# A retention, mixture and attention kernel: the first half block of the second row is loaded through ScalarE's DMA queue

## The chip, the cores and the metric

The kernel runs on one core of one Trainium2 chip. The metric is the device time of one execution in microseconds (us). The profile is a trace of one execution: PE is TensorE's matmuls and PEld its weight loads, DVE is VectorE, ACT ScalarE, POOL GpSimd; SP is SyncE, which here only issues DMA transfers. A name with a q (SPq, ACTq) is an engine's own sequencer, which among other things issues transfers.

## The reference

Three layers follow one another, all in float32, for 2 batch rows of 768 positions. The change touches the loading of the first.

```python
# 1: retention, 8 heads of 64; gamma[h] = 1 - 2 ** (-5 - h)
for t in range(S):
    state = gamma * state + einsum('bhd,bhe->bhde', k[:, :, t], v[:, :, t])
    y[:, :, t] = scale * einsum('bhd,bhde->bhe', q[:, :, t], state)
# 2: 8 experts, one per position: its own best one, or the one of the position before where local_gate >= 0.5
out[b, s] = p[e] * (maximum(x[b, s] @ w1[e], 0) @ w2[e])
# 3: 4 attention experts (causal), the top 2 of a position added with their weights
out += mask * w * ((softmax(scale * q @ k.T) @ v) @ wo[e])
```

## The kernel before

The positions are cut into 6 chunks of 128. A block n is chunk n // 2 of batch row n % 2, so blocks 0 and 1 are the first chunk of the first and of the second row, and there are 12 blocks. In memory a block is 128 partitions by 2048 floats: transposed queries, transposed keys, keys and values, 512 floats each. It is loaded in two halves of 512 KB by `load_half(n, x)` (line 244): x = 0 gives the transposed queries and keys, into a tile called `blq` in the trace, and x = 1 the keys and values, into `blk`. Each kind has four buffers. Every half is one transfer on SyncE's queue.

At the start the decay rows (`DR`, a tile whose buffer is called `am`) are loaded on ScalarE's queue (line 257); SyncE issues, in this order, the first part of the constants `K`, the first halves of blocks 0 and 1, their second halves, the rest of `K`, the first halves of blocks 2 and 3, the query table `qt`, and the second halves of blocks 2 and 3 (lines 258 to 269):

```python
        nc.scalar.dma_start(DR, drow)
        nc.sync.dma_start(K[:, :KS0], consts[:, :KS0])
        load_half(0, 0)
        load_half(1, 0)
        load_half(0, 1)
        load_half(1, 1)
        nc.sync.dma_start(K[:, KS0:], consts[:, KS0:])
```

From then on the order of every engine's instructions is the order in which they are written. For a block, `scores` (line 307 in the rows) multiplies keys by queries on PE; `fade` (line 311) multiplies the scores by the decay mask on VectorE, in two halves of 64 positions each by partition; `outputs_now` (line 349) multiplies the faded scores by the values; `state` (line 363) adds the products of decayed keys (`decay_k`, line 331, on GpSimd) and values into PSUM; `evacuate` (line 354) and `keep` (line 372) copy results out on ScalarE. From the second chunk on `outputs_past` (line 340) adds what the kept state gives for the queries that `decay_q` (line 325, on GpSimd) has scaled by `qt`. `turn_pair` (line 383) then transposes a chunk's outputs. Blocks 0 and 1 take `scores` and `fade` ahead of the loop, with a filler matmul of zeros (`busy`, line 229) between them; each pass of the loop then does `outputs_now` and `state` for two blocks, and `scores` and `fade` for the next two. A buffer is loaded again when its readers are done, and each transfer signals its landing through one of eight DMA semaphores that are given out in turn, over both queues; a transfer that reuses a semaphore first waits for the one that had it.

The pieces of the expert weights (`wraw`, line 181) are fetched on SyncE's queue from the last passes on, and layers 2 and 3 follow.

Of the kernel before, what the change touches and what calls it, by code (L numbers as in the profile page):

```python
# [108 lines left out]
def kernel(  # L109
# [14 lines left out]
    nc = tc.nc  # L124
# [115 lines left out]
    with tc.tile_pool(name="s1", bufs=2) as s1:  # L240
        XB, QT, KD, QD, AM, XR, XT, LL = {}, {}, {}, {}, {}, {}, {}, {}
        N1 = NC * B

        def load_half(n, x):
            c, b = divmod(n, B)
            XB[n, x] = s1.tile([128, 2, DM], F32, name="blk" if x else "blq", bufs=4)
            a = slice(2 * x, 2 * x + 2)
            nc.sync.dma_start(XB[n, x], blk[c, b].rearrange("p (a n) -> p a n", a=4)[:, a])

        def load_pair(c, x):  # L250
            if c >= NC:
                return
            for b in range(B):
                load_half(c * B + b, x)

        DR = s1.tile([128, H * C], F32, name="am")[0:3, :H * C // 2]
        nc.scalar.dma_start(DR, drow)
        nc.sync.dma_start(K[:, :KS0], consts[:, :KS0])
        load_half(0, 0)
        load_half(1, 0)  # L260
        load_half(0, 1)
        load_half(1, 1)
        nc.sync.dma_start(K[:, KS0:], consts[:, KS0:])
# [259 lines left out]
        with tc.manual_schedule(engines={ENG.PE, ENG.DVE, ENG.Activation, ENG.Pool, ENG.SP}):  # L523
# [82 lines left out]
            c = NC - 1  # L606
# [132 lines left out]
            for x in range(2):  # L739
                n = slice(2 * x, 2 * x + 2)  # L740
# [55 lines left out]
    with tc.tile_pool(name="mx", bufs=2) as mp:  # L796
# [44 lines left out]
        for e in range(E):  # L841
# [21 lines left out]
            for f in range(4):  # L863
# [4 lines left out]
                if N > JOIN:  # L868
                    ph = bank("B", [128, 2, CAP])
                    for a in range(2):  # L870
                        n = slice(a * 128, (a + 1) * 128)
# [6 lines left out]
                else:  # L878
                    hc = hh[:, :, 128:] if N <= 192 else None
                    hs.append((hh, hl, hc))  # L880
                    for a in range(2):
                        n = slice(a * 128, (a + 1) * 128)
# [74 lines left out]
            else:  # L957
# [39 lines left out]
                for x in range(2):  # L997
                    place(1, y1[0], x)
                    place(1, y1[1], x, True)
                    n = slice(2 * x, 2 * x + 2)  # L1000
# [496 lines left out]
```

## Time and profile before

| | us |
|---|---|
| time, median of 3 runs | 390.21 |
| lowest and highest of them | 389.69, 390.74 |
| the profiled execution | 390.05 |
| its span, from the first to the last instruction | 388.3 |
| PE busy | 377.5 |
| VectorE, ScalarE, GpSimd busy | 275.9, 237.8, 124.5 |

The span is cut into 40 slices of 9.7 us on the page; a digit is a busy share in tenths. The profiled execution has 1.75 us outside the span. The chain of work that ended last is followed back from the last instruction to whatever released each step. In the timeline a row gives a start, a duration, the engine, the line, the operation with its tiles (out<-in), a count, and in brackets the idle time of the engine just before with what ended it. In the windows each row gives a stretch, its length, busy us of PE, PEld, DVE, ACT and POOL, the granted PE clock as a share of 2.4 GHz, the mean busy share of the 16 DMA engines and the GB/s that they moved.

### The profile page before, as it was taken

To read this page: it belongs to the slowest core of one execution; us is meant where nothing else is said; L and a number is where in the kernel's file an instruction comes from. 1 tells how busy PE (TensorE), PEld (TensorE's weight loads), DVE (VectorE), ACT (ScalarE), POOL (GpSimd) and SP (SyncE) were. 2 spreads that over 40 slices of the span, in tenths; PEclk is the share of its full clock that TensorE was granted. 3 is DMA by queue.
4 is the path that set the end of the run, shared out by engine and by line. 5 is a ranking of instruction groups with operands and counts; after the bars stand their busy time and mean duration, and the time that the engine had idled before them with its cause. 6 is when DMAs were issued, how large, how long until landed. Compare 5 with 4: busy or idle time off the path is not lost.

```text
span 388.3 us, 8414 instructions
## 1 busy us (share of the span) xinstructions
PE 377.5 (97%) x2944; PEld 331.7 (85%) x2944; DVE 275.9 (71%) x783; ACT 237.8 (61%) x557; POOL 124.5 (32%) x175
## 2 busy tenths in 40 slices
PE   7999998999999999999999999999999999999994
PEld 4899996998979888898988797999889988988772
DVE  5466695885575768778888984478976876678741
ACT  1566764373465657578786882467876766759641
POOL 3744442131503013131310013535445332415420
PEclk9999998999999999999999999999999999999999
DMA  7999957477686776777777672232011101000111
GB/s 252 383 401 329 368 202 245 147 246 227 218 275 209 240 238 236 238 252 236 249 245 250 235 279 70 81 106 55 24 50 38 30 1 56 2 28 29 54 57 62
DMA packets 23609, 67.37 MB, mean 174 GB/s; under 512 B 4469, under 2 KB 4725, under 8 KB 23560
## 3 DMA queue, kind: packets, MB, share of 16 engines
q1 hardware_dynamic: 21010, 59.34, 45.0%
q0 software_dynamic: 2544, 7.42, 5.7%
q8 instruction: 25, 0.41, 0.4%
q14 instruction: 24, 0.20, 0.2%
q10 hardware_dynamic: 6, 0.01, 0.0%
HBM read 56.16 MB, written 11.07 MB: 173 GB/s over the span
## 4 chain that ended last, share of the span: by engine, by line
PE 87%; DMA 4%; DVE 3%; ACT 2%; SPq 1%; issue 1%; ACTq 0%; DVEq 0%
PE C L921 20%; PE B L873 9%; PE C L1073 8%; PE B L885 5%; PE C L1258 5%; PE B L1238 5%; PE A L1182 4%; PE C L1111 4%; PE C L1279 4%; PE A L885 3%; PE B L887 2%; DMA blq<-in_blk_dram 2%; DMA wraw<-in_w_dram 2%; PE C L917 2%; PE C L349 2%; PE A L808 2%
## 5 line engine op out<-in xcount | busy, mean ns | idle before, releaser
L191 DVE TENSOR_TENSOR wlo<-wraw,whi 128x1024 fp32r<-128x1024 f32 x64 | 76.9, 1222 | 15.7 <-ACT whi L186 15.6
L186 ACT ACTIVATE whi<-wraw 128x1024 fp32r<-128x1024 f32 x64 | 65.6, 1050 | 3.7 <-DMA wraw<-in_w_dram 3.7
L943 POOL DMA_INDIRECT x_d<-y,SI x16 | 20.1, 1253 | 128.5 <-ACT y L933 81.0
L1216 POOL TENSOR_SCALAR a<-a,mx,wt 128x128 f32<-128x128 f32 (+5 forms) x48 | 34.1, 720 | 51.3 <-PE B L1238 12.0
L1205 ACT ACTIVATE a<-a,mx 128x128 f32<-128x128 f32 (+5 forms) x48 | 32.2, 670 | 23.0 <-DVE mx L1195 19.6
L921 PE MATMUL C<-whi,hh 128*128 128x512 f32 (+4 forms) x112 | 45.5, 406 | 0.0
L921 PE MATMUL C<-whi,hl 128*128 128x512 f32 (+4 forms) x112 | 44.1, 394 | 0.0
L921 PE MATMUL C<-wlo,hh 128*128 128x512 f32 (+4 forms) x112 | 44.1, 394 | 0.0
L885 PE MATMUL B<-xx,whi 128*128 128x384 f32 (+3 forms) x100 | 31.0, 365 | 0.0
L1238 PE MATMUL B<-K,a 128*128 128x128 f32 x168 | 26.4, 274 | 0.0
L1195 DVE CUSTOM_DVE_ANT_0 a<-A,MR 128x384 f32<-128x384 f32 (+3 forms) x48 | 25.3, 531 | 1.4 <-PE A L1182 0.9
L887 PE MATMUL B<-xx,wlo 128*128 128x192 f32 (+3 forms) x100 | 25.5, 255 | 0.0
L921 PEld LDWEIGHTS C<-whi,hl 128*128 128x128 f32 (+4 forms) x112 | 20.0, 179 | 6.1
L921 PEld LDWEIGHTS C<-wlo,hh 128*128 128x128 f32 (+4 forms) x112 | 20.1, 179 | 5.0
L921 PEld LDWEIGHTS C<-whi,hh 128*128 128x128 f32 (+4 forms) x112 | 20.0, 179 | 4.7
L859 ACT ACTIVATE hh<-t 128x128 fp32r<-128x128 f32 (+4 forms) x56 | 16.3, 318 | 12.1 <-DVE t L891 10.4
L1238 PEld LDWEIGHTS B<-K,a 128*128 128x128 f32 x168 | 19.9, 140 | 2.6 <-issue 0.7
L1182 PE MATMUL A<-ks,qh 128*128 128x256 f32 (+3 forms) x56 | 21.5, 384 | 0.0
L220 POOL DMA_INDIRECT xg<-x_d,GI x14 | 16.0, 1142 | 14.8 <-DVE one L766 10.8
L1258 PE MATMUL C<-at,vv 128*64 128x256 f32 (+1 forms) x204 | 20.6, 347 | 0.0
L885 PEld LDWEIGHTS B<-xx,whi 128*128 128x128 f32 x100 | 18.8, 188 | 0.7
L887 PEld LDWEIGHTS B<-xx,wlo 128*128 128x128 f32 x100 | 19.1, 191 | 0.2
(327 smaller groups left out, 974.4 us busy)
## 6 DMA issues: line engine op xcount, KB each, us to landing
wraw<-in_w_dram SPq DMA_DIRECT2D x64, 512.0 KB, 4.0
blq<-in_blk_dram SPq DMA_DIRECT2D x12, 512.0 KB, 5.6
blk<-in_blk_dram SPq DMA_DIRECT2D x12, 512.0 KB, 10.3
x_d<-xr SPq DMA_DIRECT2D x12, 260.0 KB, 8.2
out_dram<-y SPq DMA_DIRECT2D x12, 256.0 KB, 2.0
xr<-x_d SPq DMA_DIRECT2D x10, 256.0 KB, 2.6
x_d<-ZR SPq DMA_DIRECT2D x2, 260.0 KB, 5.3
wraw<-in_wv_dram SPq DMA_DIRECT2D x1, 520.0 KB
```

The lines of the kernel that those rows point to most:

```text
L186: nc.scalar.activation(hi, raws[i], AF.Copy)
L191: nc.vector.tensor_tensor(out=lo, in0=raws.pop(i), in1=hi.bitcast(F32), op=OP.subtract)
L873: nc.tensor.matmul(ph[:, a, :N], w[:, k, n], x[:, k, :N], start=m == 0, stop=m == 11)
L885: nc.tensor.matmul(pa[:, :, :N], wh[:, k, n], XX[e][:, k, :, :N], start=k == 0, stop=False, skip_group_check=True)
L887: nc.tensor.matmul(pa[:, 1, :N], wl[:, k, n], XX[e][:, k, 0, :N], start=False, stop=k == 3, skip_group_check=True)
L921: nc.tensor.matmul(pys[i][:rows], h[:, a, n], w[:, a, :], start=f == 0 and a == 0 and m == 0, stop=f == 3 and a == 1 and m == 2)
L1073: nc.tensor.matmul(pp, w[:, k, a * 128:(a + 1) * 128], x[:, k, :], start=m == 0, stop=m == 11)
L1182: nc.tensor.matmul(ps[:, :w], qq[b, g, e][:, tq], KS[b, e][:, s0:s0 + w], start=m == 0, stop=m == 1)
L1205: nc.scalar.activation(AA[u][:, :n], AA[u][:, :n], AF.Exp, bias=mx[:, 0, i:i + 1], scale=-1.0, accum_out=mx[:, 1, i:i + 1])
L1216: nc.gpsimd.tensor_scalar(a[:, :n], a[:, :n], mx[:, 1, i:i + 1], WT[b, g][:, i, e:e + 1], op0=OP.mult, op1=OP.mult)
L1238: nc.tensor.transpose(pT[:, s - s0, :], a[:, s * C:(s + 1) * C], ident)
L1258: nc.tensor.matmul(po[j * HD:(j + 1) * HD, r], VV[b, s][:, e * HD:(e + 1) * HD], at[j][:, s, r], start=s == 0, stop=s == ns - 1, skip_grou ...
```

## The change

`load_half` gets a parameter for the queue, with SyncE's as the default, and the call for the first half of block 1 passes ScalarE's.

```diff
-        def load_half(n, x):
+        def load_half(n, x, queue=nc.sync):
             c, b = divmod(n, B)
             XB[n, x] = s1.tile([128, 2, DM], F32, name="blk" if x else "blq", bufs=4)
             a = slice(2 * x, 2 * x + 2)
-            nc.sync.dma_start(XB[n, x], blk[c, b].rearrange("p (a n) -> p a n", a=4)[:, a])
+            queue.dma_start(XB[n, x], blk[c, b].rearrange("p (a n) -> p a n", a=4)[:, a])
...
         load_half(0, 0)
-        load_half(1, 0)
+        load_half(1, 0, nc.scalar)
         load_half(0, 1)
         load_half(1, 1)
```

On ScalarE, the start of the program, as a difference (a + is a row that the changed kernel has):

```order
 L1493 UNCONDITIONAL_BRANCH [waits barrier_Pool_Activation_PE_DVE_SP_release]
 L257 DMA am<-in_drow_dram 3x512
+L248 DMA blq<-in_blk_dram 128x1024
 L354 ACT_TABLE_LOAD
 L354 ACTIVATE xT<-C 128x512 [waits PE_49] x2
```

The load stands behind the decay rows and ahead of the load of the activation table, and waits for nothing.

On SyncE's queue, the first loads before the change (a number tells tiles of one name apart: `blq_95` and `blk_99` are the halves of block 0, `blq_97` and `blk_101` those of block 1, 104 and 110 of block 2, 106 and 112 of block 3, `blq_198` is the first half of block 4; DMAHW0 to DMAHW7 are the eight DMA semaphores):

```order
L258 DMA K_63<-in_consts_dram 128x188
L248 DMA blq_95<-in_blk_dram 128x1024
L248 DMA blq_97<-in_blk_dram 128x1024
L248 DMA blk_99<-in_blk_dram 128x1024
L248 DMA blk_101<-in_blk_dram 128x1024
L263 DMA K_63<-in_consts_dram 128x268
L248 DMA blq_104<-in_blk_dram 128x1024
L248 DMA blq_106<-in_blk_dram 128x1024 [waits DMAHW0_49]
L267 DMA qt_108<-in_qtab_dram 128x512 [waits DMAHW1_49]
L248 DMA blk_110<-in_blk_dram 128x1024 [waits DMAHW2_49]
L248 DMA blk_112<-in_blk_dram 128x1024 [waits DMAHW3_49]
L248 DMA blq_198<-in_blk_dram 128x1024 [waits DMAHW4_49,PE_49]
```

And there after it:

```order
L258 DMA K_63<-in_consts_dram 128x188
L248 DMA blq_95<-in_blk_dram 128x1024
L248 DMA blk_99<-in_blk_dram 128x1024
L248 DMA blk_101<-in_blk_dram 128x1024
L263 DMA K_63<-in_consts_dram 128x268
L248 DMA blq_104<-in_blk_dram 128x1024
L248 DMA blq_106<-in_blk_dram 128x1024 [waits DMAHW0_49]
L267 DMA qt_108<-in_qtab_dram 128x512 [waits DMAHW1_49]
L248 DMA blk_110<-in_blk_dram 128x1024 [waits DMAHW2_49]
L248 DMA blk_112<-in_blk_dram 128x1024 [waits DMAHW3_49]
L248 DMA blq_198<-in_blk_dram 128x1024 [waits DMAHW4_49,PE_49]
```

Only `blq_97` has gone; what follows it moves up by one place and keeps its waits (the semaphores go round over both queues: DMAHW0 is that of the decay rows, DMAHW2 that of `blq_95`, DMAHW3 that of `blq_97`, DMAHW4 that of `blk_99`). PE, VectorE and GpSimd have the same rows in the same order.

## Rows read from the trace of the kernel before

**Rows 1.** The page: PE's busy share by slice, in tenths

```profile
PE   7999998999999999999999999999999999999994
```

**Rows 2.** Chain that ended last: start, us, what, up to 50 us

```profile
0.74 0.40 SPq L258
...
5.01 8.95 DMA blq<-in_blk_dram
...
41.50 8.16 DMA wraw<-in_w_dram
```

**Rows 3.** Timeline of the issuing queues and of ScalarE, 0 to 12 us

```profile
0.73 0.54 ACTq L257 DMA_DIRECT2D am<-in_drow_dram  x1
1.19 0.97 SPq L248 DMA_DIRECT2D blq<-in_blk_dram  x2
...
6.05 0.47 SPq L248 DMA_DIRECT2D blk<-in_blk_dram  x1
...
7.26 0.33 SPq L248 DMA_DIRECT2D blk<-in_blk_dram  x1
...
10.08 0.60 ACT L354 ACTIVATE xT<-C 128x512 f32<-128x512 f32 x1 [7.49 <-PE C L349]
```

**Rows 4.** Windows of the start: the last two numbers are DMA share and GB/s

```profile
1.50:2.00 0.50, 0.50 (x3) 0.19 (x2) 0.29 (x1) 0.50 (x1) 0.50 (x3) 1.00 0.38 82
2.00:2.50 0.50, 0.50 (x3) 0.15 (x1) 0.00 (x0) 0.50 (x1) 0.50 (x3) 1.00 0.66 221
...
2.50:5.50 3.00, 2.90 (x9) 0.58 (x7) 1.24 (x5) 0.09 (x1) 0.47 (x3) 1.00 0.95 210
5.50:10.00 4.50, 3.62 (x49) 2.92 (x49) 3.49 (x8) 0.00 (x0) 1.04 (x1) 1.00 1.02 393
...
12.00:16.00 4.00, 3.35 (x49) 2.93 (x45) 2.03 (x4) 2.79 (x8) 1.79 (x6) 1.00 1.02 406
```

**Rows 5.** Timeline of PE and of its weight loads, 5.5 to 16 us

```profile
6.00 1.16 PE L307 MATMUL A<-blq 64*128 64x128 f32 x16 [0.60 <-DMA blq<-in_blk_dram]
...
7.42 0.97 PEld L307 LDWEIGHTS C<-blq 64*128 64x128 f32 x16 [0.23 <-DMA blq<-in_blk_dram]
...
8.95 1.09 PE L349 MATMUL C<-am,blk 128*64 128x128 f32 x16 [0.37 <-DMA blk<-in_blk_dram]
10.26 1.09 PE L349 MATMUL C<-am,blk 128*64 128x128 f32 x16 [0.21 <-DMA blk<-in_blk_dram]
11.15 1.13 PE L363 MATMUL B<-blk,kd 128*64 128x64 f32 x32
...
14.09 1.16 PE L307 MATMUL C<-blq 64*128 64x128 f32 x16 [0.29 <-DMA blq<-in_blk_dram]
```

**Rows 6.** Timeline of VectorE and of GpSimd, 5 to 19 us

```profile
7.20 1.29 DVE L311 TENSOR_TENSOR am<-A,DT 128x512 f32<-128x512 f32 x2 [0.78 <-PE A L307]
8.61 1.29 DVE L311 TENSOR_TENSOR am<-C,DT 128x512 f32<-128x512 f32 x2
...
10.19 1.05 POOL L331 TENSOR_TENSOR kd<-blk,K 128x512 f32<-128x512 f32 x1 [0.18 <-DMA blk<-in_blk_dram]
...
14.68 2.50 POOL L325 TENSOR_TENSOR qd<-blq,qt 128x512 f32<-128x512 f32 x2 [2.21 <-DMA qt<-in_qtab_dram]
```

**Rows 7.** The page's DMA queues: packets, MB, share of 16 engines

```profile
q8 instruction: 25, 0.41, 0.4%
```

**Rows 8.** Timeline of PE in the second and third pass of the loop

```profile
17.17 1.95 PE L340 MATMUL C<-qd,SB 128*128 128x128 f32 x16
...
22.24 1.16 PE L307 MATMUL A<-blq 64*128 64x128 f32 x16
23.23 1.06 PE L307 MATMUL C<-blq 64*128 64x128 f32 x16
```

**Rows 9.** Windows at 40 us and at 62 to 66 us

```profile
40.00:41.00 1.00, 1.00 (x38) 0.93 (x32) 0.14 (x2) 0.60 (x1) 0.26 (x1) 1.00 0.84 270
62.00:66.00 4.00, 3.80 (x22) 2.56 (x21) 2.20 (x10) 2.34 (x5) 2.01 (x2) 0.57 0.75 273
```

## The prediction

> **What bounds the kernel now.** I read the page first: of the 40 slices all but three show PE busy for 9 tenths or more, and the first, with 7, is the lowest apart from the last [rows 1]. That first slice, about 9.7 us, is where the change lies. Next I read the chain of work that ended last, in order of time. It begins with SyncE's queue issuing its transfers back to back from 0.74 to 5.01 us, goes on with the transfer of a half block from 5.01 us to its landing at 13.96, and from there on it is PE work, beginning with the scores of block 3 at 14.09 [rows 5], until the wait for a weight transfer that is issued at 41.50 us [rows 2]. Read alone, that says "SyncE issues too slowly". Two more views say otherwise.
>
> The timeline of the queues shows what issuing costs: 0.97 us for the two first half blocks, so 0.485 us each, while the engines of the DMA need longer to move them [rows 3]. The windows show that the DMA is saturated: its share of busy time is 0.95 from 2.5 to 5.5 us and 1.02 from 5.5 to 10 and from 12 to 16 us [rows 4]. At the 393 GB/s of 5.5 to 10 us a half block of 524,288 bytes takes 1.33 us. PE's and GpSimd's waits end at that spacing: the halves of blocks 0 and 1 are there by 6.00, 7.42, 8.95 and 10.19 us, and the first half of block 3 by 14.09 [rows 5, 6]. So up to 14.09 us the DMA engines set the pace, not the issue; PE waits for them, last of all 0.29 us before the scores of block 3 [rows 5].
>
> **The change, part by part.** It moves one 512 KB transfer, the first half of block 1, from second place among SyncE's block loads to second place in ScalarE's queue. Nothing is added or removed.
>
> Step 1, ScalarE. Its queue issues the decay rows from 0.73 us for 0.54 us [rows 3]; the order shows the moved issue right behind them and ahead of a table load, which ends at 2.59 us (10.08 less the 7.49 of idling behind it, [rows 3]). No row shows a 512 KB issue on that queue; the bounds are SyncE's 0.33 us (a later one) and the 0.54 us of the small one [rows 3], and I take 0.5. The table load then ends at about 3.1 us. ScalarE's first activation starts at 10.08 us [rows 3], so this costs nothing unless the issue took 7 us.
>
> Step 2, SyncE. Everything behind the moved issue goes out up to 0.485 us earlier, as long as nothing holds it. The order shows what does: from the first half of block 3 on, each load waits for the landing of the transfer eight places ahead of it, counted over both queues. The second half of block 2 waits for the first half of block 0, and goes out at 6.05 us, right after that landing; the second half of block 3 waits for the moved transfer and goes out at 7.26 [rows 3, 5]. If the first half of block 0 lands about 1.2 us later, those two go out at about 7.2 and 7.5 us. Behind them on SyncE's queue is the first half of block 4, which is not held up: it waits for the second half of block 0, on which PE starts at 8.95 [rows 5]. The bytes of block 2's second half cannot move before the first halves of blocks 2 and 3 (14.09 us) have gone by, so 7 us of backlog hides the later issue.
>
> Step 3, who gets the DMA engines. Both queues now offer a half block from about 1.3 us on. If they don't share, the first half of block 0 still lands at 6.00; if they share evenly, both land together at about 7.42, the time at which both had landed before [rows 5]. The nearest row is the queue of instruction loads, which runs on the same engines: 0.41 MB in 0.4% of 16 x 388.3 us is 16.5 GB/s for an engine, against some 25 in the stretches of 393 and 406 GB/s over 16 [rows 4, 7]. It loses speed to the other queue, so I take sharing: 7.2 us, a little before 7.42 because SyncE issues 0.1 us earlier.
>
> The Trainium skill (DMA: Bandwidth & Descriptors, "Issuing engines are not separate DMA queues") says that transfers started by different engines run on the same 16 DMA engines and interleave, and that starting them from several engines saves no more than the issuing time. Applied here, the most that the change could bring would be rival (a) below, and S in step 4 would be near the shared end; the spacing of 1.33 us against 0.485 us in the rows agrees that issuing is the smaller of the two.
>
> Step 4, PE's chain from that landing. Call the start of the scores of block 0 S (6.00 before). The first fade starts 1.20 us later and takes 1.29; the scores of block 1 can follow PE's filler at about S + 1.19 (PE reached them 0.23 us before 7.42) and need 1.19 to their fade, so the second fade starts at S + 2.49, when VectorE is free, and ends at S + 3.78 [rows 5, 6]. From block 1's output matmuls to the state is 0.89 us (10.26 to 11.15) and 1.13 more to the next scores, 2.02 in all; the scores of block 3 follow 0.99 us behind those of block 2 where no data is missing (22.24 to 23.23) [rows 5, 8]. So PE is ready for the scores of block 3 at S + 6.79. They started at 14.09, so **a later landing costs nothing up to S = 7.30**, and one for one beyond. With S = 7.2 PE is ready at 13.99. The cover here is PE's waits for half blocks, of 0.37, 0.21 and 0.29 us among others [rows 5]; they are used up, and what is late next is PE itself.
>
> Step 5, when the last of these loads lands. The bytes before block 3 are the same, so its landing moves only if idle DMA time at the start is filled. From 2.0 to 2.5 us the share is 0.66, idle for 0.17 us; from 1.5 to 2.0 it is 0.38, idle for 0.31 [rows 4]. The bounds are 0 and 0.48; I take 0.17, since the earlier idling lies before the first data of any block. That gives 14.09 - 0.17 = 13.92.
>
> **Sum.** The scores of block 3 start at the later of 13.92 and 13.99: 0.10 us earlier. Between the bounds (S from 6.00 to 7.42, landing 0 to 0.48 earlier) this is from 0.48 earlier to 0.12 later. From there the chain is PE [rows 2], so the shift is carried. At 41.50 us it runs through a weight transfer, whose issue waits for PE's state matmuls; the DMA share of 0.84 at 40 to 41 us says there is no backlog that would swallow it [rows 2, 9]. The transform of block 2's queries waits for a table until 14.68 and ends, for blocks 2 and 3 together, at 17.18; the matmuls that read it start at 17.17 with block 2's own half, so 0.1 us fits [rows 6, 8]. The profiled execution took 390.05 us (388.3 span), 0.16 below the median of 390.21: 390.05 - 0.10 = 389.95, and for a median 390.1.
>
> **Rivals.** (a) *The issue does bound the start*, as the chain of waits reads: all that follows goes out 0.485 us earlier and lands so, with S at or below 6.8. For it: the chain. Against it: the DMA share near 1. It gives 389.7.
> (b) *Two queues hide each other's slow packets.* From 2.5 to 5.5 us the engines are 0.95 busy but move 210 GB/s, against 393 later [rows 4]. If the second queue fills that, 3.0 x (1 - 210/393) = 1.4 us are gained and the scores of block 3 start near 12.7, which PE can follow (S = 5.9 gives 12.69): 388.8. Against it: the engines are shown busy, not idle, in that stretch, and the moved bytes go through the same ones.
> (c) *Slower: sharing delays block 0's half past 7.30 us.* Place: the scores of block 0. It decides from S = 7.30 and costs 1 us per us. If three half blocks shared the engines until 8.95 us, S is 8.95 and the loss 1.65: 391.9. For it: the slow packets of 2.5 to 5.5 us may grow with a second stream. A loss over 1.17 us needs S above 8.47.
> (d) *The transfer is not ahead where it should be*: ScalarE's queue is served behind SyncE's, so block 1's half lands after the fourth, at 10.19. Then its scores start 2.77 us later, its fade ends at 12.67 instead of 9.90, and scores of block 3 start at 12.67 + 2.02 + 0.99 = 15.68, a loss of 1.6: 391.8. Against it: the instruction queue's packets do get their share.
>
> **How the numbers follow.** About 0.3% (1.17 us) is what a measurement can tell from no change. Chances: forecast 62%, (a) 14%, (b) 8%, (c) 13%, (d) 3%. Forecast, (a) and the lower two thirds of (c) are within 0.3%; (b) is faster; the upper end of (c) and (d) are slower. That is 8% faster, 86% same, 6% slower. Runs of the kernel before went from 389.69 to 390.74, half a us either way, so the range takes (a) at 389.7 less 0.4 and the lower half of (c) at about 391: 389.3 to 391.0. Left out are (b), (d) and the upper part of (c).
>
> **What would show it.** In the profile after: ScalarE's issue at about 1.3 us for 0.5; the scores of block 0 starting near 7.2 instead of 6.00 and those of block 1 about 1.2 later without a wait; output matmuls of block 1 near 11 instead of 10.26; scores of block 3 within 0.3 us of 14.09. Scores of block 0 still at 6.00 would refute the sharing; scores of block 3 before 13.5 us would mean (a) or (b); after 15 us (c) or (d). The clock is granted at half (1.2 GHz) for a part of 62 to 66 us, the mean being 0.57 [rows 9]; if that stretch changed its length, the time would change for a reason outside this argument.

## The result and the profile after

The changed kernel takes 393.67 us (median of 7 runs, the fastest 390.42), the kernel before 390.21 (7 runs, 389.69 to 391.79): slower by 0.63%, the ratio being 1.0063 with an interval of 1.0042 to 1.0085. One run of 532.09 us, whose mean granted clock was 0.66, is not in the ratio, and without it the median is 393.15 us. 390.1 with a range of 389.3 to 391.0 had been forecast, so the forecast was wrong: 0.63% of 390.21 is 2.5 us, more than the 1.17 us of no change.

The profiled execution of the changed kernel is its fastest one, of 390.42 us. Its page looks almost like the one of before [rows 1]. The rows to look at are the clock's and that of q10, ScalarE's queue. Before the change they are:

```profile
PEclk9999998999999999999999999999999999999999
...
q10 hardware_dynamic: 6, 0.01, 0.0%
```

After it the clock's row has an 8 in the first slice and none near 62 us (the seventh slice), and q10, which carried little more than the decay rows, now carries the moved half block:

```profile
PEclk8999999999999999999999999999999999999998
...
q10 hardware_dynamic: 150, 0.53, 0.5%
```

The issues went as forecast in steps 1 and 2 [rows 3]. ScalarE's queue issues the load at 1.32 us in 0.37, and the second halves of blocks 2 and 3 go out behind the landing of block 0's half, at 7.02 us:

```profile
1.32 0.37 ACTq L248 DMA_DIRECT2D blq<-in_blk_dram  x1
...
7.02 1.07 SPq L248 DMA_DIRECT2D blk<-in_blk_dram  x2
...
9.16 1.04 POOL L331 TENSOR_TENSOR kd<-blk,K 128x512 f32<-128x512 f32 x1 [6.20 <-DMA blk<-in_blk_dram]
```

GpSimd gets the second halves of blocks 0 and 1 at 9.16 and 10.39 us, 0.2 later than before [rows 6]. PE's timeline is where the time goes; the rows that answer to [rows 5] are:

```profile
4.23 1.04 PE L229 MATMUL B<-WZ 128*128 128x512 bf16 x4
7.04 1.98 PE L307 MATMUL A<-blq 64*128 64x128 f32 x16 [1.77 <-DMA blq<-in_blk_dram]
8.95 0.61 PE L229 MATMUL B<-WZ 128*128 128x512 bf16 x1
9.49 1.67 PE L307 MATMUL C<-blq 64*128 64x128 f32 x16
...
15.49 1.06 PE L307 MATMUL C<-blq 64*128 64x128 f32 x16
```

Block 0's scores start at 7.04 us (forecast 7.2, before 6.00). But the 16 matmuls of them take 1.98 us instead of 1.16, the filler 0.61 instead of 0.39, block 1's scores 1.67, and block 3's scores start at 15.49 instead of 14.09. The windows of the same execution say why (the number ahead of the last two is the granted clock):

```profile
5.00:7.00 2.00, 0.27 (x2) 0.00 (x0) 1.28 (x5) 0.00 (x0) 0.00 (x0) 1.00 0.93 326
7.00:9.00 2.00, 1.96 (x17) 1.74 (x17) 0.00 (x0) 0.00 (x0) 0.00 (x0) 0.55 1.02 398
9.00:11.00 2.00, 2.00 (x19) 1.54 (x17) 1.29 (x2) 0.00 (x0) 1.65 (x2) 0.60 1.04 412
11.00:13.00 2.00, 1.86 (x30) 1.52 (x28) 1.29 (x2) 0.60 (x1) 1.67 (x6) 1.00 1.03 412
...
60.00:70.00 10.00, 8.65 (x80) 6.80 (x77) 6.69 (x28) 4.42 (x15) 2.00 (x2) 1.00 0.65 214
```

From 5.27, the end of the filler (4.23 + 1.04), to 7.04 PE has nothing to do. Then the granted clock is at its lower level, 1.2 GHz, for most of 7 to 11 us (a mean of 0.55 and 0.60), and at 2.4 GHz again from 11 on. In the kernel before the filler ended at 5.41 (4.37 + 1.04), PE idled until 6.00 [rows 5], and the scores took 1.16 us:

```profile
4.37 1.04 PE L229 MATMUL B<-WZ 128*128 128x512 bf16 x4
```

The chain of work that ended last now runs through the later landing of block 0's half, right behind its issue, and straight on through the slow matmuls:

```profile
1.19 5.81 DMA blq<-in_blk_dram
...
7.04 1.98 PE A L307 x16
```

### The profile page after: what moved, and what is told of

Its sections match the earlier page's. It is cut to its first block, busy times and chain, and to the rows that moved or that the text cites. A ratio compares the mean times of both kernels' runs of the same rounds, so it can differ in the third digit from the quotient of the medians.

```text
span 388.6 us, 8414 instructions
## 1 busy us (share of the span) xinstructions
PE 377.3 (97%) x2944; PEld 331.8 (85%) x2944; DVE 275.1 (71%) x783; ACT 237.8 (61%) x557; POOL 123.1 (32%) x175
## 3 DMA queue, kind: packets, MB, share of 16 engines
q0 software_dynamic: 2544, 7.42, 5.7%
## 4 chain that ended last, share of the span: by engine, by line
PE 87%; DVE 5%; DMA 4%; ACT 2%; issue 1%; SPq 0%; ACTq 0%; DVEq 0%
PE C L921 20%; PE B L873 9%; PE C L1073 7%; PE B L885 5%; PE C L1258 5%; PE B L1238 5%; PE A L1182 4%; PE C L1111 4%; PE C L1279 4%; PE A L885 3%; PE B L887 2%; DMA wraw<-in_w_dram 2%; PE C L917 2%; PE C L349 2%; PE A L808 2%; DMA blq<-in_blk_dram 1%
```

## The experiments

Two theories stood against each other. The **clock theory**: PE idles longer because block 0's half lands later, and the clock is down when the first blocks are worked on. The **DMA theory**: transfers land later further on, because of the second queue. To tell them apart I used, for every trace, the same marks: the start of block 0's and of block 3's scores, of the gate matmuls of the last chunk (line 644), of the first expert matmul (line 873) and of the last output matmuls (line 1304). They are gathered in the table behind the last experiment.

**The changed kernel again**, with timed runs.

> The changed kernel once more, unaltered, for a second trace and its time. Two theories. Clock theory: the scores of block 0 start near 7.0 us after PE idled from 5.3, TensorE's granted clock falls to half for about 3.4 us, and the scores of block 3 start near 15.5 us instead of 14.09; the rest of the loss is a further half-clock stretch near 62 us, which the first trace of the changed kernel lacked; span 390.5 to 392, time 392 to 394. DMA theory: the granted clock is 1.00 up to 60 us, and the loss comes from transfers that land later between 14 and 70 us. If the first trace (388.6) is the typical one, the time is 390.4.

Median 392.33 us in 10 runs (390.65 to 393.5) against 390.21, ratio 1.0052 (1.0030 to 1.0074): the loss repeats. Its profiled execution (390.77 us) has block 0's scores at 7.05 us taking 2.08, and block 3's at 15.46:

```profile
4.62 1.89 PE L229 MATMUL B<-WZ 128*128 128x512 bf16 x4
7.05 2.08 PE L307 MATMUL A<-blq 64*128 64x128 f32 x16 [0.54 <-DMA blq<-in_blk_dram]
```

Two things went against the expectation. This execution has no half-clock stretch near 62 us either. And PE did not idle from 5.3 us: the filler itself ran at half rate (1.89 us against 1.04) until 6.51, and PE waited 0.54 us, no longer than in the kernel before. So here the rate was low ahead of the wait, and the wait did not lower it.

**More filler behind the decay masks**, to bridge the wait:

```diff
-        busy(pB, WARM // 2)
+        busy(pB, WARM // 2 + 8)
         pTab = pB[:, :2 * E].rearrange("p (i e) -> p i e", i=2)
```

> The changed kernel with 8 more filler matmuls of zeros (1.7 us at full clock) behind the decay masks, so that PE is busy until the half block lands near 7.0 us. Clock theory: the granted clock stays at 1.00 from 4 to 16 us, the scores of block 0 take 1.16 us again, the scores of block 3 start between 13.9 and 14.3 us, and the time is that of the kernel before, 390.2 within 0.5. DMA theory: as slow as the changed kernel, 392 to 394.

It was slower still: 393.59 us, ratio 1.0084 (1.0051 to 1.0118). The row of the filler shows my mistake:

```profile
4.62 5.30 PE L229 MATMUL B<-WZ 128*128 128x512 bf16 x12
9.85 1.28 PE L307 MATMUL A<-blq 64*128 64x128 f32 x16
```

5.30 us for 12 recorded filler matmuls is 0.44 us each, against 0.26 for the 4 that took 1.04 us at 4.23 above. In this execution they ran at half rate, the filler lasted until 9.85 us, and it delayed what it should have kept fast. Filler of a fixed count is cheap at one clock and a delay at the other. The clock theory's forecast of 390.2 us failed, and the time is in the DMA theory's range; but with the filler as a delay of its own, and one trace for four runs, the run decides nothing between the two.

**The kernel before without the filler behind the masks**: an idle PE, no transfer moved.

```diff
-        busy(pB, WARM // 2)
         pTab = pB[:, :2 * E].rearrange("p (i e) -> p i e", i=2)
```

> The kernel before, all loads on SyncE's queue, without the 5 filler matmuls behind the decay masks: PE idles from about 4.4 us to the landing at 6.0, about as long as in the changed kernel (1.8 us), but no transfer is moved. Clock theory: in runs whose granted clock falls, it falls near 7 us for about 3.4 us, the scores of block 3 start up to 1 us later than 14.09 and the time is 391 to 393; in runs where it does not fall, 390.2. DMA theory: 390.2, since no transfer differs.

```profile
3.24 1.03 PE L288 MATMUL B<-am,ONB 3*128 3x512 bf16 x2
...
6.20 2.08 PE L306 MATMUL A<-blq 64*128 64x128 f32 x16 [1.93 <-DMA blq<-in_blk_dram]
...
15.14 1.06 PE L306 MATMUL C<-blq 64*128 64x128 f32 x16
```

Here line 306 is line 307 of the others. The half lands at about the time of before (6.20), PE has idled 1.93 us, and the scores run at half rate; block 3's start at 15.14, and the time is 391.18, ratio 1.0019 (1.0002 to 1.0036). So a slow start costs time without any moved load, though less than the change. That the idling made it slow is not shown by this trace: the two matmuls on the decay rows (line 288), ahead of the idling, took 1.03 us, as in the execution of 390.77 us with its slow filler, while in traces with a fast filler they took 0.60 to 0.98.

**The two first halves in the other order, both on SyncE's queue**: a late landing without a second queue.

```diff
-        load_half(0, 0)
         load_half(1, 0)
+        load_half(0, 0)
```

> The kernel before with the first halves of blocks 0 and 1 issued in the other order, both on SyncE's queue: the half of block 0 lands at about 7.3 us, as in the changed kernel, without a second queue. Clock theory: PE idles until 7.3 us as there, and it is as slow as the changed kernel, 392 to 394. DMA theory (the second queue is to blame): 390.2 to 390.5.

```profile
4.62 1.89 PE L229 MATMUL B<-WZ 128*128 128x512 bf16 x4
7.19 2.08 PE L307 MATMUL A<-blq 64*128 64x128 f32 x16 [0.69 <-DMA blq<-in_blk_dram]
...
16.44 0.83 PE L307 MATMUL C<-blq 64*128 64x128 f32 x11
```

Landing near 7.2 us, half-rate scores, block 3's scores at 16.44, 392.11 us, ratio 1.0046 (1.0017 to 1.0076). That is about the changed kernel's loss without its queue, and the DMA theory falls with it: a late landing of block 0's half is enough. How it lowers the rate this trace doesn't show, since the filler is slow already and PE waits only 0.69 us.

**Further traces of both kernels unaltered**, one execution each.

> The kernel before, unaltered, for a second trace of it. Clock theory: TensorE's granted clock is at full from some point near 4 us on and stays so until 58 us; the scores of block 0 start near 6.0 us, those of block 3 within 0.3 of 14.09; a half-clock stretch of 3.4 us, or none, between 60 and 70 us; time 389.3 to 391.9. If the scores of block 3 start 1 us or more after 14.09 although the load is not moved, the start of the kernel before is as unsteady as that of the changed one, and the theory loses its ground.

> The changed kernel, unaltered, for a third trace of it, wanted from an execution of 392 us or more. Clock theory: scores of block 0 near 7.05 us at half clock, scores of block 3 at 15.4 to 16.5 us, 45.6 us from there to the gate matmuls of the last chunk as in every trace so far, and a half-clock stretch between 60 and 70 us that makes the rest; no time lost after 71 us.

The kernel before took 389.07 us:

```profile
5.97 1.16 PE L307 MATMUL A<-blq 64*128 64x128 f32 x16 [0.66 <-DMA blq<-in_blk_dram]
...
13.40 1.16 PE L307 MATMUL C<-blq 64*128 64x128 f32 x16 [0.34 <-DMA blq<-in_blk_dram]
```

The changed kernel took, by luck, 389.25 us, and this trace differs from all others of it:

```profile
6.59 1.16 PE L307 MATMUL A<-blq 64*128 64x128 f32 x16 [0.98 <-DMA blq<-in_blk_dram]
...
8.00 1.16 PE L307 MATMUL C<-blq 64*128 64x128 f32 x16
...
13.48 1.06 PE L307 MATMUL C<-blq 64*128 64x128 f32 x16
```

```profile
7.00:9.00 2.00, 2.00 (x31) 1.63 (x27) 1.22 (x2) 0.00 (x0) 0.00 (x0) 1.00 1.01 389
```

Same kernel, same queues; block 0's scores start at 6.59, the scores take 1.16 us, and block 3's start at 13.48 us, 0.08 behind the kernel before's 13.40 in the trace above. In this one execution, in which the clock held, the change cost next to nothing; but block 0's half also came earlier than in the other traces of the changed kernel, and the two effects are not separated here. A later trace, of 391.70 us, shows another start with a slow filler:

> The changed kernel, unaltered, for a fourth trace, wanted from an execution of 392 us or more. Clock theory, for any time that it shows: scores of block 3 at 13.5 us if the granted clock stays at full from 4.5 us on, and at 15.4 us or later if not; 45.6 us from there to the gate matmuls; 308.5 us from the first matmul of the experts to the last matmuls.

```profile
4.62 1.89 PE L229 MATMUL B<-WZ 128*128 128x512 bf16 x4
7.07 2.08 PE L307 MATMUL A<-blq 64*128 64x128 f32 x16 [0.56 <-DMA blq<-in_blk_dram]
...
9.62 2.08 PE L307 MATMUL C<-blq 64*128 64x128 f32 x16
...
16.02 1.06 PE L307 MATMUL C<-blq 64*128 64x128 f32 x16
```

```profile
7.00:9.00 2.00, 1.94 (x16) 1.78 (x16) 0.00 (x0) 0.00 (x0) 0.00 (x0) 1.00 1.02 393
```

Here, as in the execution of 390.77 us, the filler before the scores is slow already (1.89 us for the 4 recorded, against 1.04), and both blocks' scores run at half rate behind it, while the column of the granted clock reads 1.00. Block 3's start at 16.02.

**The second queue with block 0's half unharmed.** The load on ScalarE's queue waits until ScalarE has written ones into its buffer:

```diff
+            if queue is not nc.sync:
+                nc.scalar.activation(XB[n, x][:, 0], ONES[:, :1].to_broadcast([128, DM]), AF.Copy)
             queue.dma_start(XB[n, x], blk[c, b].rearrange("p (a n) -> p a n", a=4)[:, a])
```

> The changed kernel, with the moved load issued at about 3.2 us instead of 1.32: ScalarE first writes zeros or ones into its buffer, and the load waits for that. ScalarE's queue is still used, but the half of block 0 has most of the engines to itself. Clock theory: it lands near 6.0 to 6.3 us again, the granted clock does not fall, the scores of block 3 start within 0.5 us of 14.09, and the time is 389.7 to 390.8. If a second queue costs time by itself, 392 to 393.

Block 0's half did land at 5.99 us, but the time was 393.85, ratio 1.0088 (1.0061 to 1.0115), which I had not expected:

```profile
3.28 0.38 ACTq L250 DMA_DIRECT2D blq<-in_blk_dram  x1
```

```profile
5.99 1.16 PE L309 MATMUL A<-blq 64*128 64x128 f32 x16 [0.74 <-DMA blq<-in_blk_dram]
...
10.43 1.99 PE L309 MATMUL C<-blq 64*128 64x128 f32 x16 [2.95 <-DMA blq<-in_blk_dram]
```

```profile
9.00:11.00 2.00, 0.57 (x6) 0.60 (x8) 0.00 (x0) 0.00 (x0) 1.61 (x3) 0.89 1.03 310
11.00:13.00 2.00, 2.00 (x20) 1.77 (x19) 0.61 (x2) 0.00 (x0) 0.67 (x4) 0.50 0.99 342
```

(Line 309 is line 307 of the others.) Issued at 3.28 us, the half block landed at 10.29, 7 us later: three half blocks of SyncE's queue were ahead of it and served first (PE had the first at 5.99, GpSimd the others at 7.38 and 9.39). PE idled 2.95 us before block 1's scores, and the clock fell again, now ahead of 11 us. So this run missed its aim, a second queue without a gap, and showed a low clock behind a long wait at another place.

**Another load on ScalarE's queue**, the first part of the constants, in the kernel before:

```diff
-        nc.sync.dma_start(K[:, :KS0], consts[:, :KS0])
+        nc.scalar.dma_start(K[:, :KS0], consts[:, :KS0])
         load_half(0, 0)
```

> The kernel before, with another load moved: the first part of the constants (94 KB) goes to ScalarE's queue behind the decay rows, so that SyncE issues the half of block 0 first, at 0.74 instead of 1.19 us. Clock theory: the half lands 0.2 to 0.5 us before 6.0, PE idles shorter, and the time is that of the kernel before or up to 0.6 us below: 389.6 to 390.3. If sharing with the constants delays it past 6.5 us instead, 391 or more.

Block 0's half came at 5.68 us, as hoped, but the median was 391.24, ratio 1.0025 (1.0003 to 1.0048). VectorE shows the cause:

```profile
7.42 2.16 DVE L291 SCALAR_TENSOR_TENSOR DT<-B,K 128x128 f32<-128x128 f32 x8 [5.62 <-DMA K<-in_consts_dram]
```

The 94 KB, issued at 1.32 us, reached VectorE at 7.42, so the decay masks, until then off the path, came 3 us late, PE idled 1.95 us behind them, and the granted clock was at 0.50 from 11 to 13.5 us.

**Filler ahead of the decay masks instead**, in the changed kernel and, as a control, in the kernel before:

```diff
-        busy(pB, WARM // 2)
+        busy(pB, WARM // 2 + 4)
         for j, ps in enumerate((pS.rearrange("p b a n -> p (b a n)"), pR)):
```

> The changed kernel with 4 more filler matmuls ahead of the decay masks (0.43 us each at half clock), where VectorE has 0.8 us to spare; the masks come later, so PE idles about 0.9 us instead of 1.8 before the half block lands near 7 us. The transfers are those of the changed kernel. Clock theory: the granted clock is at full more often when block 0's scores start, the scores of block 3 start at 13.5 to 14.3 us in most executions, and the median falls to 389.7 to 391.0. If the clock is not the cause, the median stays at 392 to 393.

> The control: the same 4 filler matmuls in the kernel before. PE then idles for 0 to 0.3 us before block 0's half, and the masks end near 7.1 us, just ahead of the first fade. Clock theory: 389.5 to 390.4, as the kernel before or a little faster, since late clock rises become rarer; and the changed kernel with the filler within 0.5 us of it, which would say that the queue itself costs nothing.

Changed kernel: 391.18 us in 12 runs (388.54 to 392.96), ratio to the kernel before 1.0026 (1.0005 to 1.0048), about half the loss, and just above the 389.7 to 391.0 of the expectation. Its profiled execution:

```profile
7.17 1.16 PE L307 MATMUL A<-blq 64*128 64x128 f32 x16 [0.98 <-DMA blq<-in_blk_dram]
...
14.06 1.06 PE L307 MATMUL C<-blq 64*128 64x128 f32 x16
```

Block 0's scores start even later, at 7.17, but at full clock, and block 3's start at 14.06. The control: 389.90 us, ratio 0.9987 (0.9964 to 1.0011), from 388.34 to 391.85; its profiled execution is one of its longer ones (391.63 us), in which the filler ran at half rate and held block 0's scores until 8.14 (block 3's: 15.92). So a start at half rate occurs without a moved load, too. The two with filler are still 1.3 us apart, not within 0.5, so that the queue costs nothing is not shown by them.

**A last try to beat both**: the kernel before with 9 filler matmuls ahead of the masks and 1 behind.

> The kernel before with the filler in front of the decay masks instead of behind them: 9 filler matmuls ahead and 1 behind (before: 5 and 5). Where the clock rises late, the trace with 9 and 5 showed block 0's scores waiting for the filler until 8.14 us; with 1 behind they start near 6.4 there, and the scores of block 3 near 14.3 instead of 15.9; where it rises early nothing changes. Clock theory: median 389.0 to 389.9 with no group of runs at 391.7. If more filler at the front doesn't make the early rise more frequent, 390.0 to 391.

390.07 us, ratio 0.9997 (0.9979 to 1.0015), with two of the 12 runs at 391.54 and 391.78, so the expectation of 389.0 to 389.9 failed. No gain; no version here beats the kernel before.

**The changed kernel near its median.** The traces so far stopped at 391.70 us, while the medians were 392.3 and 393.2; where the rest of the loss lies was open. Three more executions, unaltered:

> The changed kernel unaltered, one execution, to catch one near its median of 392.3 to 393.7 us. Clock theory: block 3's scores start at 15.4 to 16.5 us when the early matmuls run at half clock, the stretch from there to line 644 is again 45.6 and the last 308.5, and any time beyond 391.7 us is a longer half-clock stretch between 60 and 73 us, with a lower mean granted clock (0.991 or less). DMA theory: the excess lies in a stretch with the clock at full, behind a late landing.

> The same once more. Clock theory: of two executions the slower one has the lower mean granted clock, and the difference between them is found in the stretch up to block 3's scores and in the one from line 644 to the first expert matmul, nowhere else. DMA theory: it is found elsewhere.

> The same a third time. Clock theory: as in the other two; with block 3's scores at 16 and a stretch of 12.4 us from line 644 to the first expert matmul the time would be about 393. DMA theory: a time above 392 us with both stretches as in the execution of 390.42 us.

They took 391.93, 390.63 and 395.12 us. Part of what was expected failed: the mean granted clock of the first is 0.993, not 0.991 or less, and not below the 0.992 of the second, which is faster. In the first the filler and the scores ran at half rate while the column read 1.00, so the mean doesn't count them. The first two are otherwise like those before; the third is slower than any of them:

```profile
1.19 6.93 DMA blq<-in_blk_dram
```

```profile
8.16 2.08 PE L307 MATMUL A<-blq 64*128 64x128 f32 x16 [2.78 <-DMA blq<-in_blk_dram]
...
10.71 2.08 PE L307 MATMUL C<-blq 64*128 64x128 f32 x16
...
17.27 1.06 PE L307 MATMUL C<-blq 64*128 64x128 f32 x16
```

```profile
64.00:66.00 2.00, 2.00 (x21) 2.00 (x22) 0.75 (x4) 0.03 (x1) 0.00 (x0) 0.86 0.82 287
66.00:68.00 2.00, 1.83 (x13) 1.75 (x14) 1.06 (x7) 0.59 (x2) 1.00 (x1) 0.50 0.71 283
...
70.00:72.00 2.00, 2.00 (x6) 0.86 (x6) 1.28 (x6) 0.00 (x0) 0.00 (x0) 0.50 0.38 114
72.00:74.00 2.00, 2.00 (x17) 1.87 (x16) 1.92 (x8) 0.60 (x4) 0.00 (x0) 0.93 0.37 137
```

The landing of block 0's half comes at 8.12 us, 6.93 after its issue (first line, from the chain that ended last), a us or more later than in the other six, with the same issues. PE idles 2.78 us before it, the scores of both blocks and the filler between them run at half rate, and block 3's scores start at 17.27 instead of 14.09. At 64 to 74 us the clock is low again, 0.50 on the mean from 66 to 72, and so for twice as long as in the kernel before [rows 9].

**All traces side by side** (us from the span's start; "low" says at which of the early steps matmuls ran at half rate):

| kernel | block 0's scores | low | block 3's scores (A) | line 644 (B) | first expert matmul (C) | line 1304 (D) | B - A | C - B | D - C |
|---|---|---|---|---|---|---|---|---|---|
| before | 6.00 | no | 14.09 | 59.83 | 70.91 | 379.4 | 45.74 | 11.08 | 308.5 |
| before, second trace | 5.97 | no | 13.40 | 59.11 | 70.12 | 378.5 | 45.71 | 11.01 | 308.4 |
| changed | 7.04 | scores 0, 1 | 15.49 | 61.27 | 71.48 | 379.8 | 45.78 | 10.21 | 308.3 |
| changed, again | 7.05 | filler, scores 0, 1 | 15.46 | 61.02 | 71.18 | 380.2 | 45.56 | 10.16 | 309.0 |
| changed, 389.25 us | 6.59 | no | 13.48 | 59.05 | 69.99 | 378.6 | 45.57 | 10.94 | 308.6 |
| changed, 391.70 us | 7.07 | filler, scores 0, 1 | 16.02 | 61.58 | 72.73 | 381.1 | 45.56 | 11.15 | 308.4 |
| changed, 391.93 us | 7.14 | filler, scores 0, 1 | 16.09 | 61.65 | 72.90 | 381.4 | 45.56 | 11.25 | 308.5 |
| changed, 390.63 us | 7.09 | scores 0, 1 | 15.54 | 61.10 | 71.63 | 380.0 | 45.56 | 10.53 | 308.4 |
| changed, 395.12 us | 8.16 | scores 0, 1 | 17.27 | 63.59 | 75.98 | 384.5 | 46.32 | 12.39 | 308.5 |
| more filler behind | 9.85 | filler | 16.87 | 63.43 | 75.79 | 384.2 | 46.56 | 12.36 | 308.4 |
| no filler behind | 6.20 | scores 0, 1 | 15.14 | 60.71 | 71.86 | 380.6 | 45.57 | 11.15 | 308.7 |
| other order | 7.19 | filler, scores 0, 1 | 16.44 | 62.00 | 73.02 | 381.5 | 45.56 | 11.02 | 308.5 |
| late second queue | 5.99 | scores 1 | 16.94 | 62.50 | 73.60 | 382.1 | 45.56 | 11.10 | 308.5 |
| constants moved | 5.68 | outputs of 0, 1 | 16.30 | 61.86 | 72.85 | 381.4 | 45.56 | 10.99 | 308.6 |
| changed, filler ahead | 7.17 | no | 14.06 | 59.62 | 70.68 | 379.3 | 45.56 | 11.06 | 308.6 |
| before, filler ahead | 8.14 | filler, scores 0 | 15.92 | 61.48 | 72.41 | 381.0 | 45.56 | 10.93 | 308.6 |
| before, 9 and 1 | 6.30 | no | 13.49 | 59.16 | 70.14 | 378.8 | 45.67 | 10.98 | 308.7 |

From A to B all but two traces take 45.6 to 45.8 us, and from C to D all take 308.3 to 309.0. So in these traces what a kernel loses before block 3's scores it keeps to the end, and one later stretch, from B to C, adds a term of its own. The windows at 60 to 74 us tell which: where the granted clock is 1.00 throughout (the changed kernel's 390.42, 390.77 and 390.63), it takes 10.2 to 10.5 us; with a low stretch of 3 to 4 us, as in the kernel before [rows 9], 10.9 to 11.3; with the long ones of the 395.12 us execution and of the run with more filler, 12.4.

## Why the prediction was wrong

Step 1 held: the issue took 0.37 us (0.5 taken) and hides in ScalarE's idling. Step 2 held: the second halves of blocks 2 and 3 go out at 7.02 us and later, and no one waits for them.

Step 3 held mostly: block 0's scores start at 7.04 to 7.14 us in five traces, 7.2 being forecast, at 6.59 in one and at 8.16 in one. So sharing is what happens, with a spread that one number did not carry. The other order on one queue gives 7.19: what counts is that the engines carry two half blocks first.

**Step 4 is the step that failed.** Its chain is right at full clock: 6.79 us was worked out from block 0's scores to block 3's, and the two traces in which this chain binds show 6.89 (13.48 - 6.59, and 14.06 - 7.17). With it a start at 7.04 gives 13.93, and the forecast of no loss. But the durations in it were those of a trace in which the clock was up. Where the first scores ran at the lower clock the chain took 8.41 to 8.95 us in five traces of the changed kernel (15.49 - 7.04 = 8.45), and 9.11 in the slowest (17.27 - 8.16). So the term that was missing is 1.6 to 2.3 us. PE's waits were called cover that can be used up, and a longer wait of PE ahead of block 0 was priced at nothing. The clock was looked at only at 62 to 66 us [rows 9] and put outside the argument, and no rival carried it.

Two kinds of start lead to that lower rate, and only one of them shows the wait as its cause. In three traces of the changed kernel (390.42, 390.63 and 395.12 us) the filler ran at full rate (1.04 us), PE then waited 1.77, 1.78 and 2.78 us, and the granted clock fell to 0.50 after 7 us. The Trainium skill has a rule for this (TensorE: Matmul & The Clock Gate, "Part 1: The HAM clock gate"): the clock is set by how busy PE has lately been, and after idling it falls to 1.2 GHz. The traces with a fast filler agree: the low clock followed these three waits, and 2.95 us in the run with the late queue and 1.95 with the constants moved, and did not follow 0.98 in the execution of 389.25 us.

In the other three (390.77, 391.70 and 391.93 us) the filler was at half rate already (1.89 us), and PE waited 0.54 to 0.63 us, about as long as in the kernel before (0.60). There the wait did not lower the rate; it had not yet risen. The run with the other order and the control with filler ahead started so without a load on the second queue, and up to block 0's landing PE has the same work in both kernels, so nothing shows that the change makes such starts. What they cost the kernel before is open, since neither of its two traces is one. The later landing may prolong them: in the two traces that went on from the filler into the scores without a wait (more filler behind; before, filler ahead) block 1's scores ran at full rate, and in the four with a wait of 0.54 to 0.69 us they took 1.54 to 2.08; this is a hint and no test.

Step 5 can't be judged. Block 3's half was there by 13.48 us in the execution of 389.25 us, earlier than the 13.92 of the step, but by 13.40 in the second trace of before as well; the 0.69 us between the two traces of before (14.09 and 13.40) is more than the 0.17 that the step argued about.

The sum: the shift is carried to the end, as written (B - A and D - C above). In the profiled execution 1.40 us are lost at block 3's scores and 0.87 given back from B to C, because the low stretch near 62 us is missing there; so that execution is only 0.37 us slower, while its kernel's median is 2.9 slower (393.15 against 390.21). In the execution of 395.12 us everything is paid, against the profiled one of before: 3.18 us up to block 3's scores, 0.58 more up to B and 1.31 from B to C, together 5.07, which is its whole difference (395.12 - 390.05). That the stretch near 62 us could change for reasons outside the argument was said; that it does so together with the start was not.

Of the rivals, (c) had the direction and, in the slowest execution, its condition: 8.16 is past 7.30. There it explains 0.86 us by its own price, and the lower clock the other 2.3 of 3.18. In five of the other six traces its condition was not met and A is late all the same, so its mechanism is not the main one. (a) and (b) fall with the start of block 0's scores and of block 3's. (d) did not happen in the changed kernel: block 1's half was there when PE reached it. It did happen in the run with the late queue. The chances, added up as the prediction says, are 85% for the same and 7% for slower, not 86 and 6; nothing hangs on it.

What stays open: how often each of these starts occurs, and how the loss of the median divides between them. Seven traces of the changed kernel have a median of 390.77 us, its timed runs 392.3 and 393.2, and no execution between 391.93 and 395.12 was traced, where most of the timed runs lie. That the lower rate makes up the loss there too is argued from the traces on either side. Filler ahead speaks for it, which with the same transfers brought the ratio from 1.0052 and 1.0063 down to 1.0026, though the intervals overlap. Why the half block took a us longer in one execution, and why the stretch from A to B then grew by 0.6, was not followed further. That the second queue costs nothing by itself is not shown; for it speak one execution, that of 389.25 us, and the other order on one queue, which loses 0.46% without it; the run that should have shown it alone, with the late queue, made a gap of its own.

## What to carry to other kernels

A wait of TensorE is not free cover just because other work ends the stage: before moving a load, ask how long PE will idle ahead of it and price the matmuls that follow at half the clock, too (here 1.6 to 2.3 us). Look first whether the matmuls ahead of the wait ran at full rate. The second queue here gave a transfer a share of the same engines, taken from the transfer that was first; the one needed first should have them to itself. When a profile is that of the fastest run, compare its marks with those of a second and third execution before explaining a median by it.

## What the runs showed of the hardware

The same kernel starts in different ways with the same instructions. The 4 filler matmuls of 512 columns after the decay rows take 1.04 us in some executions and 1.89 in others. The column of the granted clock reads 1.00 at the start all the same (from 0 to 16 us in the execution of 391.93 us, with 1.89 for the filler and 2.08 for the scores of either block); there only the durations of the matmuls show the low rate.

The start goes with what the clock does 45 us later; why is open. With block 3's scores at 15.46 to 15.54 us there was no low stretch at 60 to 74 us (three traces of three); with earlier and with later starts there was one, and the two longest belong to two of the three latest starts (16.87 and 17.27).

A half block on ScalarE's queue, issued together with SyncE's, landed 6.3 to 7.0 us after its issue; issued 2 us later, behind three others, it still took 7.0. Half of the 274 GB/s that moved from 2.5 to 5.5 us there would have brought it in 3.8 us (an estimate), so it did not get half of what the engines moved.
